# One PSUM bank for two heads' scores, and the FFN weights' residuals moved from GpSimd to VectorE

## The chip, the cores and the metric

The kernel runs on one core of a Trainium2 chip. A core has five engines that work beside each other, each through its own queue in order: TensorE (PE in the profile, with PEld for its weight loads), VectorE (DVE), ScalarE (ACT), GpSimd (POOL) and SyncE (SP), which here issues the DMAs. SBUF is the working memory; PSUM holds what PE writes, in banks of 512 fp32 columns on 128 partitions. The metric is the time of one execution in microseconds; the median of several executions is compared.

## What is computed

Three layers one after the other on 8 sequences of 576 tokens and 512 channels, all in fp32:

```python
# attention: 8 heads of 64, blocks of 64 positions, causal by block
scores = np.where(block_i >= block_j, q @ k.T / 8, -1e9)
x = softmax(scores) @ v                      # heads side by side: 576 x 512
# gated causal convolution of 5 taps
x = (sigmoid(conv5(x)) * (x @ w_val)) @ w_out
# Fourier mixing and a feed-forward layer
u = x + real(fft(fft(x, axis=1), axis=2))
un = (u - mean(u)) / sqrt(var(u) + 1e-6)
out = u + relu(un @ w_ch1) @ w_ch2           # 512 -> 2048 -> 512
```

## The kernel before

Products that must be exact to more than one rounded fp32 format are split: a value is rounded to a high part (`H`), the residual is its low part (`L`), and PE adds three matmuls, high x high, high x low and low x high.

`phase1` does attention, the gate and the Fourier stages. Its unit `n` is one of nine per head pair `p` (`p, i = divmod(n, NB)`): for `i` below 8 it is head `i % 2` and query tile `i // 2` of 128 queries; `i = 8` is the last 64 queries of both heads. A loop over `n` writes, in each round, the scores of unit `n` (`emit_qk`, two matmuls into a PSUM tile that `sc_tile` hands out), its masked maximum (`emit_max`), its exponents (`emit_exp`, on ACT, into `PB[i]`), six units later the transposes of the exponents (`emit_t`, line 487) and the product with `v` (`emit_av`, line 509). A score tile is one bank; three banks named `sc` go round (in the first 36 units two further ones help). Pieces of `dense`, the projections `psv` and `psx` and the Fourier matmuls of a batch of four head pairs, are strewn in between so that PE has work. Small stages that evacuate PSUM hang in chains that are run a step per round.

```python
t = sc_tile(n)
q = QQ[h][i // 4]
nc.tensor.matmul(t[:, 0:w], q[:, 0, m], KK[p][h][:, 0:w], start=True, stop=False)
nc.tensor.matmul(t[:, 0:w], q[:, 1, m], KL[p][:, 0:w], start=False, stop=True)
```

With `w = max(256, L)` and `L` 128 or 256, the first four units of a pair use half of their bank.

`phase2` is the feed-forward layer, in nine groups of 512 tokens. It reads the two weight matrices as 64-bit numbers; `load_w(f)` brings one of 16 slices of each as a raw tile `rw` (three buffers) and decodes it: three integer steps on DVE (lines 72, 74, 76) build the fp32 bits in `st` (three buffers), ACT takes the absolute value `mg` (line 80), DVE clears what is too small (line 84). Then ACT rounds `st` to `W1H` or `W2H` (line 962) and GpSimd subtracts to get `W1L` or `W2L` (line 963). `norm(g)` sums the four channel tiles of `U`, subtracts the mean, splits `x` into `UTH` and `UTL` (line 1015) and adds the squares `q` (line 1019). For each hidden tile `f`, PE makes `psh` from `W1` (lines 1049 to 1051), ACT the rectified high part `hh` (line 1054), DVE the low part `hl` (line 1055), and PE adds `W2` times both into four banks `o` (lines 1067 to 1069), one tile behind `psh`. In group 0 the decode of tile `f + 2` is written ahead of hidden tile `f`; `norm(g + 1)` runs inside group `g`. At a group's end DVE scales `o` and GpSimd adds it to `U` (line 1078).

The order on each queue is not that of the source: the tile framework's scheduler arranges the instructions of the whole program by its own estimate of when each can run, and places the semaphores. A queue waits in order, so an instruction that waits holds all behind it.

Of the kernel before, what the change touches and what calls it, by code (L numbers as in the profile page):

```python
# [8 lines left out]
F32 = mybir.dt.float32  # L9
F32R = mybir.dt.float32r  # L10
AF = mybir.ActivationFunctionType
ALU = mybir.AluOpType
AX = mybir.AxisListType
# [4 lines left out]
def kernel(  # L18
# [13 lines left out]
    nc = tc.nc  # L32
    B, NP, P, S = q.shape
# [66 lines left out]
    def phase1():  # L100
        with ExitStack() as c1:
# [4 lines left out]
            px, pv, pg, pool = (c1.enter_context(tc.tile_pool(name=f"p{n}", bufs=1)) for n in "xvgz")  # L106
# [12 lines left out]
            QQ = [[pa.tile([P, 2, 256], F32R, name=f"QQ{h}{g}") for g in range(2)] for h in range(2)]  # L119
# [23 lines left out]
            o = [0]  # L143
# [166 lines left out]
            qraw, kraw, KK, KP, KL, VV = {}, {}, {}, {}, {}, {}  # L310
# [62 lines left out]
                                      in_=QHL[rs[h], 0:1, c].bitcast(F32).to_broadcast([64, 2, 256]))  # L373
                    nc.sync.dma_start(out=QQ[h][g][rs[1 - h], 0, :].bitcast(F32), in_=QHL[rs[h], 1, c].bitcast(F32))

            sums, scs, maxs = {}, {}, {}

            sc_at = [0]

# [6 lines left out]

            def emit_qk(n):
                p, i = divmod(n, NB)
                if i < 8:

                    h, L = i % 2, P * (i // 2 + 1)
                    w = max(256, L)
                    m = slice(P * (i // 2 % 2), P * (i // 2 % 2) + P)
                    t = sc_tile(n)
                    q = QQ[h][i // 4]
                    nc.tensor.matmul(t[:, 0:w], q[:, 0, m], KK[p][h][:, 0:w], start=True, stop=False)  # L396
                    nc.tensor.matmul(t[:, 0:w], q[:, 1, m], KL[p][:, 0:w], start=False, stop=True)  # L397
                    scs[n] = [(t[:, 0:L], 0, L)]
                    return

                sc = []
                for k0, w in ((0, 320), (320, 256)):
                    t = sc_tile(n)
                    mm3(t[:, 0:w], QD[p % 2][:, 0], QD[p % 2][:, 1], KP[p][:, k0:k0 + w], KL[p][:, k0:k0 + w], True, True)
                    sc.append((t[:, 0:w], k0, w))
                scs[n] = sc

            def emit_max(n):
                sc = scs[n]
                mx = sm.tile([P, 4], F32, tag="mx", name="mx")  # L410
                one = len(sc) == 1
                if one:

                    L = sc[0][2]
                    nc.vector.memset(sc[0][0][0:64, L - 64:L], -1e9)
                for j, (t, k0, w) in enumerate(sc):
                    nc.vector.reduce_max(out=mx[:, j:j + 1], in_=t, axis=AX.X, negate=one)  # L417
                if not one:
                    nc.vector.reduce_max(out=mx[:, 2:3], in_=mx[:, 0:2], axis=AX.X, negate=True)
                maxs[n] = mx[:, 0:1] if one else mx[:, 2:3]  # L420
# [488 lines left out]
    def phase2():  # L909
        with ExitStack() as c2:  # L910
# [39 lines left out]
            def load_w(f):  # L950
                for src, h, l in (
                    (w_ch1[:, f * P:(f + 1) * P].bitcast(I32).rearrange("(c p) f -> p c f", p=P), W1H[f], W1L[f]),
                    (w_ch2[f * P:(f + 1) * P, :].bitcast(I32), W2H[f], W2L[f]),
                ):
                    rw = rp.tile([P, 2 * D], I32, tag="r", name="rw")
                    nc.sync.dma_start(out=rw if h is W2H[f] else rw.rearrange("p (c f) -> p c f", c=4), in_=src)
                    if h is W1H[f]:
                        h, l = h.rearrange("p c f -> p (c f)"), l.rearrange("p c f -> p (c f)")
                    st = s3.tile([P, D], F32, tag="st", name="st")
                    for stage in decode(rw, st, s4.tile([P, D], F32, tag="mg", name="mg")):  # L960
                        stage()
                    nc.scalar.copy(out=h, in_=st)  # L962
                    nc.gpsimd.tensor_tensor(out=l, in0=st, in1=h.bitcast(F32), op=ALU.subtract)  # L963

            U, UTH, UTL, RS = {}, {}, {}, {}

# [28 lines left out]
            def norm(g):  # L995
# [3 lines left out]
                UTH[g] = UHS[g % 2]  # L999
                UTL[g] = ULS[g % 2]  # L1000
                u = U[g]
                s1 = s2.tile([P, T], F32, tag="x", name="s1")
                s = s2.tile([P, T], F32, tag="x", name="s")
                nc.vector.tensor_tensor(out=s1, in0=u[:, 2, :], in1=u[:, 3, :], op=ALU.add)
                nc.gpsimd.tensor_tensor(out=s, in0=u[:, 0, :], in1=u[:, 1, :], op=ALU.add)
                nc.vector.tensor_tensor(out=s, in0=s, in1=s1, op=ALU.add)
                yield
                pm = ps_t.tile([P, T], F32, tag="t", name="pm")
# [2 lines left out]
                for t in range(4):  # L1011
                    x = s2.tile([P, T], F32, tag="x", name="x")
                    nc.vector.tensor_tensor(out=x, in0=u[:, t, :], in1=pm, op=ALU.subtract)
                    nc.scalar.copy(out=UTH[g][:, t, :], in_=x)
                    (nc.gpsimd if g and t % 2 else nc.vector).tensor_tensor(
                        out=UTL[g][:, t, :], in0=x, in1=UTH[g][:, t, :].bitcast(F32), op=ALU.subtract)
                    nc.scalar.activation(out=x if t else q, in_=x, func=AF.Square)
                    if t:
                        nc.gpsimd.tensor_tensor(out=q, in0=q, in1=x, op=ALU.add)
                    yield  # L1020
                pv = ps_t.tile([P, T], F32, tag="t", name="pv")
                yield from average(g, pv, q)
# [154 lines left out]
```

## Time and profile before

| | |
|---|---|
| median of three executions | 1527.51 us (1521.43 to 1528.04) |
| the profiled execution | 1526.26 us, of which the span of the trace is 1524.5 |
| TensorE | 1449.9 us busy, 95% of the span |
| VectorE | 859.1 us, 56% |
| ScalarE | 666.4 us, 44% |
| GpSimd | 393.1 us, 26% |
| granted TensorE clock, mean | 0.986 of full speed |

A busy share over the whole span hides that the stretches differ, so the rows below are asked for stretch by stretch. A duration is that of one instruction; on an engine with full work the distance from one start to the next is a little shorter than the duration, and it is this distance (the pitch) that adds up.

### The profile page before, as it was taken

To read this page: it belongs to the slowest core of one execution; us is meant where nothing else is said; L and a number is where in the kernel's file an instruction comes from. 1 tells how busy PE (TensorE), PEld (TensorE's weight loads), DVE (VectorE), ACT (ScalarE), POOL (GpSimd) and SP (SyncE) were. 2 spreads that over 40 slices of the span, in tenths; PEclk is the share of its full clock that TensorE was granted. 3 is DMA by queue.
4 is the path that set the end of the run, shared out by engine and by line. 5 is a ranking of instruction groups with operands and counts; after the bars stand their busy time and mean duration, and the time that the engine had idled before them with its cause. 6 is when DMAs were issued, how large, how long until landed. Compare 5 with 4: busy or idle time off the path is not lost.

```text
span 1524.5 us, 22867 instructions
## 1 busy us (share of the span) xinstructions
PE 1449.9 (95%) x8300; PEld 1213.1 (80%) x8300; DVE 859.1 (56%) x1798; ACT 666.4 (44%) x1674; POOL 393.1 (26%) x350
## 2 busy tenths in 40 slices
PE   4799999999999999988889999999999999999998
PEld 3477888888888888886667888888888888888887
DVE  6878797969796969599994222223222321322212
ACT  5678777777777777724342212112121211212110
POOL 3423332324232323245443112011111101111100
PEclk9899999999999999999999999999999999999999
DMA  7566555555454545224441010010101001010000
GB/s 205 159 166 186 145 143 131 143 133 147 125 148 121 153 116 137 87 74 136 144 137 56 1 52 4 1 56 0 56 0 55 1 2 53 0 56 1 28 1 28
DMA packets 114272, 129.12 MB, mean 85 GB/s; under 512 B 20208, under 2 KB 87792, under 8 KB 114160
## 3 DMA queue, kind: packets, MB, share of 16 engines
q1 hardware_dynamic: 114160, 127.67, 29.6%
q8 instruction: 66, 1.08, 0.3%
q14 instruction: 46, 0.38, 0.1%
HBM read 62.61 MB, written 18.87 MB: 53 GB/s over the span
## 4 chain that ended last, share of the span: by engine, by line
PE 80%; DVE 10%; DMA 3%; issue 3%; ACT 3%; POOL 1%; SPq 1%; DVEq 0%; ACTq 0%; POOLq 0%
PE o L1069 8%; PE o L1067 8%; PE o L1068 8%; PE psh L1050 8%; PE psh L1051 8%; PE psh L1049 8%; PE av L509 6%; PE pt L487 5%; PE sc L396 3%; PE sc L397 2%; PE psx L160 2%; PE psx L162 2%; PE psx L161 2%; DVE st L76 2%; PE psv L160 2%
## 5 line engine op out<-in xcount | busy, mean ns | idle before, releaser
L1055 DVE SCALAR_TENSOR_TENSOR hl<-psh,hh 128x512 fp32r<-128x512 f32 x144 | 99.2, 689 | 398.9 <-ACT hh L1054 398.9
L1054 ACT ACTIVATE hh<-psh 128x512 fp32r<-128x512 f32 x144 | 85.7, 595 | 494.8 <-PE psh L1051 494.8
L1069 PE MATMUL o<-hl,W2H 128*128 128x512 f32 x576 | 226.9, 395 | 16.6 <-DVE hl L1055 16.6
L1051 PE MATMUL psh<-UTH,W1L 128*128 128x512 f32 x576 | 224.7, 390 | 2.0 <-POOL W1L L963 2.0
L1067 PE MATMUL o<-hh,W2H 128*128 128x512 f32 x576 | 226.0, 393 | 0.0
L1068 PE MATMUL o<-hh,W2L 128*128 128x512 f32 x576 | 225.7, 392 | 0.0
L1049 PE MATMUL psh<-UTH,W1H 128*128 128x512 f32 x576 | 224.4, 390 | 0.3 <-ACT W1H L962 0.3
L1050 PE MATMUL psh<-UTL,W1H 128*128 128x512 f32 x576 | 224.2, 389 | 0.0
L430 ACT ACTIVATE PB<-sc,mx 128x128 f32<-128x128 f32 (+4 forms) x320 | 167.0, 524 | 47.9 <-DVE mx L417 40.8
L487 PE MATMUL pt<-ident,PB 128*128 128x128 f32 x800 | 139.1, 279 | 11.3 <-ACT PTb L492 4.2
L417 DVE TENSOR_REDUCE mx<-sc 128x1 f32<-128x128 f32 (+4 forms) x320 | 148.0, 473 | 2.7
L1069 PEld LDWEIGHTS o<-hl,W2H 128*128 128x128 f32 x576 | 109.1, 190 | 43.5 <-DVE hl L1055 21.0
L540 DVE SCALAR_TENSOR_TENSOR gate<-XF,cw,gate 128x575 f32<-128x575 f32 (+3 forms) x128 | 135.0, 1055 | 1.4 <-ACT gate L63 0.5
L1051 PEld LDWEIGHTS psh<-UTH,W1L 128*128 128x128 f32 x576 | 108.1, 188 | 25.5 <-POOL W1L L963 2.9
L1068 PEld LDWEIGHTS o<-hh,W2L 128*128 128x128 f32 x576 | 109.3, 190 | 22.9
L1067 PEld LDWEIGHTS o<-hh,W2H 128*128 128x128 f32 x576 | 109.1, 189 | 23.0 <-ACT hh L1054 0.2
L1049 PEld LDWEIGHTS psh<-UTH,W1H 128*128 128x128 f32 x576 | 108.4, 188 | 23.4 <-ACT W1H L962 0.7
L1050 PEld LDWEIGHTS psh<-UTL,W1H 128*128 128x128 f32 x576 | 108.1, 188 | 22.5
L396 PE MATMUL sc<-K,QQ 128*128 128x256 f32 (+2 forms) x256 | 92.6, 363 | 26.1 <-DMA QQ<-QHL 13.0
L487 PEld LDWEIGHTS pt<-ident,PB 128*128 128x128 f32 x800 | 99.5, 142 | 21.0 <-ACT PTb L492 7.1
L1078 POOL TENSOR_TENSOR U<-o,U 128x512 f32<-128x512 f32 x32 | 40.3, 1292 | 273.9 <-DVE o L1076 273.9
L492 ACT COPY PTb<-pt 128x512 f32<-128x512 f32 (+1 forms) x192 | 92.8, 501 | 31.2 <-PE pt L487 29.9
(184 smaller groups left out, 2931.7 us busy)
## 6 DMA issues: line engine op xcount, KB each, us to landing
K<-KP SPq DMA_DIRECT2D x128, 144.0 KB, 2.5
QQ<-QHL SPq DMA_DIRECT2D x128, 128.0 KB, 2.4
rw<-in_w_ch SPq DMA_DIRECT2D x32, 512.0 KB, 3.9
VV<-in_v SPq DMA_DIRECT2D x32, 320.0 KB, 3.8
qraw<-in_q SPq DMA_DIRECT2D x32, 288.0 KB, 3.0
kraw<-in_k SPq DMA_DIRECT2D x32, 288.0 KB, 3.1
out<-U SPq DMA_DIRECT2D x36, 256.0 KB, 2.0
QQ<-QHL SPq DMA_DIRECT2D x128, 64.0 KB, 2.1
```

The source lines that it names most:

```text
L396: nc.tensor.matmul(t[:, 0:w], q[:, 0, m], KK[p][h][:, 0:w], start=True, stop=False)
L417: nc.vector.reduce_max(out=mx[:, j:j + 1], in_=t, axis=AX.X, negate=one)
L430: nc.scalar.activation(out=PB[i][:, k0:k0 + w], in_=t, func=AF.Exp, bias=nm, accum_out=su[:, i + j:i + j + 1])
L487: nc.tensor.transpose(ps[:, j, :], PB[i][:, (j0 + j) * P:(j0 + j + 1) * P], ident)
L540: nc.vector.scalar_tensor_tensor(out=gate[c][:, s:S], in0=XF[:, 0:S - s], scalar=cw[:, c, 4 - s:5 - s], in1=gate[c][:, s:S], op0=ALU.mult, ...
L1049: nc.tensor.matmul(ps, W1H[f][:, c, :], UTH[g][:, c, :], start=(c == 0), stop=False)
L1050: nc.tensor.matmul(ps, W1H[f][:, c, :], UTL[g][:, c, :], start=False, stop=False)
L1051: nc.tensor.matmul(ps, W1L[f][:, c, :], UTH[g][:, c, :], start=False, stop=(c == 3))
L1055: nc.vector.scalar_tensor_tensor(out=l, in0=ps, scalar=0.0, in1=h.bitcast(F32), op0=ALU.max, op1=ALU.subtract)
L1067: nc.tensor.matmul(po[t], W2H[e][:, c], h, start=(e == 0), stop=False)
L1068: nc.tensor.matmul(po[t], W2L[e][:, c], h, start=False, stop=False)
L1069: nc.tensor.matmul(po[t], W2H[e][:, c], l, start=False, stop=(e == NF - 1))
```

## The change

Two things are changed. In `phase1`, the unit of head 0 (`i` 0 and 2) also does the scores of head 1, in the second half of the same bank; `emit_qk` of `i` 1 and 3 does nothing; one memset and one maximum with two results serve both heads, and `emit_max` of the second returns at once. The exponents stay one per head. In `phase2`, the residuals `W1L` and `W2L` are subtracted on DVE, and in `norm` of groups 0 and 1 the sum, the residuals `UTL` and the sum of squares are on DVE too; from group 2 on they stand where they stood.

```diff
             def emit_qk(n):
                 p, i = divmod(n, NB)
+                if i in (1, 3):
+
+                    return
                 if i < 8:
...
-                    q = QQ[h][i // 4]
-                    nc.tensor.matmul(t[:, 0:w], q[:, 0, m], KK[p][h][:, 0:w], start=True, stop=False)
-                    nc.tensor.matmul(t[:, 0:w], q[:, 1, m], KL[p][:, 0:w], start=False, stop=True)
-                    scs[n] = [(t[:, 0:L], 0, L)]
+                    for u in range(2 if i < 4 else 1):
+                        h, o = (u, w * u) if i < 4 else (i % 2, 0)
+                        q = QQ[h][i // 4]
+                        nc.tensor.matmul(t[:, o:o + w], q[:, 0, m], KK[p][h][:, 0:w], start=True, stop=False)
+                        nc.tensor.matmul(t[:, o:o + w], q[:, 1, m], KL[p][:, 0:w], start=False, stop=True)
+                        scs[n + u] = [(t[:, o:o + L], 0, L)]
+                    if i < 4:
+                        twos[n] = t.rearrange("p (h w) -> p h w", h=2)[:, :, 0:L]
...
             def emit_max(n):
+                if n in maxs:
+                    return
...
+                if n in twos:
+                    t = twos.pop(n)
+                    L = sc[0][2]
+                    nc.vector.memset(t[0:64, :, L - 64:L], -1e9)
+                    nc.vector.reduce_max(out=mx[:, 0:2], in_=t, axis=AX.X, negate=True)
+                    maxs[n], maxs[n + 1] = mx[:, 0:1], mx[:, 1:2]
+                    return
...
                     nc.scalar.copy(out=h, in_=st)
-                    nc.gpsimd.tensor_tensor(out=l, in0=st, in1=h.bitcast(F32), op=ALU.subtract)
+                    nc.vector.tensor_tensor(out=l, in0=st, in1=h.bitcast(F32), op=ALU.subtract)
...
+                pool = nc.gpsimd if g > 1 else nc.vector
...
-                nc.gpsimd.tensor_tensor(out=s, in0=u[:, 0, :], in1=u[:, 1, :], op=ALU.add)
+                pool.tensor_tensor(out=s, in0=u[:, 0, :], in1=u[:, 1, :], op=ALU.add)
...
-                    (nc.gpsimd if g and t % 2 else nc.vector).tensor_tensor(
+                    (pool if t % 2 else nc.vector).tensor_tensor(
...
-                        nc.gpsimd.tensor_tensor(out=q, in0=q, in1=x, op=ALU.add)
+                        pool.tensor_tensor(out=q, in0=q, in1=x, op=ALU.add)
```

On PE's queue, at the start of a head pair in the third batch, the scores of the two heads' first query tiles (`sc`, 128x256) stood eight rows apart before (`K_3395` is head 0, `K_3396` head 1; `PB` 119 and 120 are exponents of the pair ahead):

```order
L396 MATMUL sc<-K_3395,QQ_112 128x256
L397 MATMUL sc<-KL,QQ_112 128x256
L487 MATMUL pt<-ident,PB_119 128x128 x2
L160 MATMUL psv<-XH_132,wv_h 128x288
L161 MATMUL psv<-XL_137,wv_h 128x288
L162 MATMUL psv<-XH_132,wv_l 128x288
L160 MATMUL psv<-XH_133,wv_h 128x288
L161 MATMUL psv<-XL_138,wv_h 128x288
L162 MATMUL psv<-XH_133,wv_l 128x288
L396 MATMUL sc<-K_3396,QQ_114 128x256
L397 MATMUL sc<-KL,QQ_114 128x256
L487 MATMUL pt<-ident,PB_120 128x128 x3
```

and now (line numbers are those of the changed source):

```order
L401 MATMUL sc<-K_3291,QQ_112 128x256
L402 MATMUL sc<-KL,QQ_112 128x256
L401 MATMUL sc<-K_3292,QQ_114 128x256
L402 MATMUL sc<-KL,QQ_114 128x256
L503 MATMUL pt<-ident,PB_119 128x128 x2
L160 MATMUL psv<-XH_132,wv_h 128x288
L161 MATMUL psv<-XL_137,wv_h 128x288
L162 MATMUL psv<-XH_132,wv_l 128x288
L160 MATMUL psv<-XH_133,wv_h 128x288
L161 MATMUL psv<-XL_138,wv_h 128x288
L162 MATMUL psv<-XH_133,wv_l 128x288
L503 MATMUL pt<-ident,PB_120 128x128 x3
```

The second head's two matmuls moved up behind the first head's; the rows around them kept their order, and the next score tile is taken ten rows after the last one shown.

On DVE's queue, in the decode of two weight slices of group 0, before:

```order
L76 SCALAR_TENSOR_TENSOR st<-rw,st 128x512 x2
L84 SCALAR_TENSOR_TENSOR st<-mg,st 128x512 x2
L1055 SCALAR_TENSOR_TENSOR hl_9419<-psh,hh_9417 128x512
L72 TENSOR_SCALAR st<-rw 128x512
L1013 TENSOR_TENSOR x<-U_9485,pm 128x512
```

and now:

```order
L72 TENSOR_SCALAR st<-rw 128x512 x2
L74 SCALAR_TENSOR_TENSOR st<-rw,st 128x512 x2
L76 SCALAR_TENSOR_TENSOR st<-rw,st 128x512 x2
L84 SCALAR_TENSOR_TENSOR st<-mg,st 128x512 x2
L1073 SCALAR_TENSOR_TENSOR hl_9164<-psh,hh_9162 128x512
L979 TENSOR_TENSOR W1L_9202<-st,W1H_9201 128x512
L979 TENSOR_TENSOR W2L_9204<-st,W2H_9203 128x512
```

The two residuals moved into DVE's queue, behind the `hl` of an earlier hidden tile and ahead of the next slice's first step.

On ACT's queue in the same place, before:

```order
L962 CAST W1H_9457<-st 128x512
L80 ACTIVATE mg<-rw 128x512
L1054 ACTIVATE hh_9417<-psh 128x512
L962 CAST W2H_9459<-st 128x512
L80 ACTIVATE mg<-rw 128x512
```

and now:

```order
L1072 ACTIVATE hh_9161<-psh 128x512
L978 CAST W1H_9193<-st 128x512
L80 ACTIVATE mg<-rw 128x512
L978 CAST W2H_9195<-st 128x512
L80 ACTIVATE mg<-rw 128x512
L1072 ACTIVATE hh_9162<-psh 128x512
L978 CAST W1H_9197<-st 128x512
```

`hh`, which reads what PE made, moved ahead of the first of the two roundings.

## Rows read from the trace of the kernel before

**Rows 1.** Stretches, core 0: length, busy PE, PEld, DVE, ACT, POOL (count), PEclk, DMA, GB/s

```profile
100.00:657.00 557.00, 543.96 (x4187) 474.70 (x4182) 447.56 (x1164) 415.26 (x1168) 181.29 (x173) 1.00 0.51 136
657.00:717.00 60.00, 50.13 (x292) 43.52 (x291) 57.93 (x89) 24.39 (x47) 30.84 (x21) 0.94 0.28 96
717.00:804.00 87.00, 71.04 (x287) 54.90 (x286) 87.00 (x117) 36.88 (x64) 37.90 (x27) 0.96 0.45 149
804.00:1524.00 720.00, 715.71 (x3148) 591.60 (x3148) 194.28 (x252) 125.27 (x213) 106.66 (x79) 1.00 0.07 24
```

**Rows 2.** PE's waits, 100 to 650 us: total us, times, longest

```profile
PE sc L396 <- ACT PB L430: 11.8, 12, 2.4
```

**Rows 3.** Timeline 280 to 284 us, ACT and PE: start, length, [idle before <-releaser]

```profile
280.06 0.68 ACT L340 ACTIVATE QHL<-qraw 128x576 fp32r<-128x576 f32 x1 [1.67 <-DMA K<-KP]
...
281.30 0.39 PE L396 MATMUL sc<-K,QQ 128*128 128x256 f32 x1 [1.34 <-ACT PB L430]
...
281.64 0.49 PE L487 MATMUL pt<-ident,PB 128*128 128x128 f32 x3
...
283.89 0.30 PE L161 MATMUL psv<-XL,wv_h 128*128 128x288 f32 x1
```

**Rows 4.** DVE's groups by shape, 100 to 650 us: busy us, mean ns | idle before

```profile
L417 DVE TENSOR_REDUCE mx<-sc 128x1 f32<-128x512 f32 x54 | 37.1, 688 | 1.1
L417 DVE TENSOR_REDUCE mx<-sc 128x1 f32<-128x256 f32 x81 | 33.3, 411 | 0.2
...
L415 DVE MEMSET sc<- 64x64 f32 x215 | 24.0, 112 | 35.7 <-PE sc L397 28.3 <-PE pt L487 2.2 <-ACT KP L57 1.7
L417 DVE TENSOR_REDUCE mx<-sc 128x1 f32<-128x128 f32 x54 | 14.8, 274 | 0.0
```

**Rows 5.** PE's waits, 657 to 804 us

```profile
PE o L1069 <- DVE hl L1055: 16.6, 9, 3.2
```

**Rows 6.** DVE's groups by shape, 657 to 804 us

```profile
L76 DVE SCALAR_TENSOR_TENSOR st<-rw,st 128x512 int32<-128x512 int32 x32 | 32.6, 1027 | 0.0
L84 DVE SCALAR_TENSOR_TENSOR st<-mg,st 128x512 f32<-128x512 f32 x32 | 29.4, 926 | 0.0
L74 DVE SCALAR_TENSOR_TENSOR st<-rw,st 128x512 int32<-128x512 int32 x32 | 28.7, 903 | 0.0
L72 DVE TENSOR_SCALAR st<-rw 128x512 int32<-128x512 int32 x32 | 19.0, 602 | 0.0
```

**Rows 7.** Timeline of DVE, 718 to 722 us

```profile
718.48 0.41 DVE L72 TENSOR_SCALAR st<-rw 128x512 int32<-128x512 int32 x1
718.81 1.79 DVE L76 SCALAR_TENSOR_TENSOR st<-rw,st 128x512 int32<-128x512 int32 x1
720.52 0.68 DVE L74 SCALAR_TENSOR_TENSOR st<-rw,st 128x512 int32<-128x512 int32 x1
721.12 0.68 DVE L84 SCALAR_TENSOR_TENSOR st<-mg,st 128x512 f32<-128x512 f32 x1
```

**Rows 8.** Timeline of POOL, 718 to 722 us

```profile
718.68 1.37 POOL L963 TENSOR_TENSOR W2L<-st,W2H 128x512 fp32r<-128x512 f32 x1 [2.22 <-ACT W2H L962]
```

**Rows 9.** POOL's groups by shape, 657 to 804 us

```profile
L746 POOL TENSOR_TENSOR XA<-XA 128x580 f32<-128x580 f32 x6 | 9.7, 1616 | 5.9 <-DVE XA L746 5.9
```

**Rows 10.** ACT's groups by shape, 717 to 804 us

```profile
L80 ACT ACTIVATE mg<-rw 128x512 f32<-128x512 f32 x23 | 15.4, 669 | 1.5 <-DMA rw<-in_w_ch 1.5
...
L962 ACT CAST W1H<-st 128x512 fp32r<-128x512 f32 x12 | 7.4, 620 | 28.9 <-DVE st L84 28.9
L1054 ACT ACTIVATE hh<-psh 128x512 fp32r<-128x512 f32 x11 | 6.4, 579 | 0.0
```

**Rows 11.** Timeline of PE, 797 to 804 us

```profile
797.30 0.39 PE L1049 MATMUL psh<-UTH,W1H 128*128 128x512 f32 x1
797.53 0.39 PE L1050 MATMUL psh<-UTL,W1H 128*128 128x512 f32 x1
...
803.84 0.75 PE L1069 MATMUL o<-hl,W2H 128*128 128x512 f32 x1 [3.20 <-DVE hl L1055]
```

More of the change, by code (lines that the diff above doesn't have):

```diff
@@ L374, in spread @@
                     nc.sync.dma_start(out=QQ[h][g][rs[1 - h], 0, :].bitcast(F32), in_=QHL[rs[h], 1, c].bitcast(F32))
-            sums, scs, maxs = {}, {}, {}
+            sums, scs, maxs, twos = {}, {}, {}, {}
             sc_at = [0]
@@ L388, in emit_qk @@
                 p, i = divmod(n, NB)
+                if i in (1, 3):
+                    return
                 if i < 8:
-                    h, L = i % 2, P * (i // 2 + 1)
+                    L = P * (i // 2 + 1)
                     w = max(256, L)
```

## The prediction, made before the changed kernel was run

> **What bounds the kernel now.** I read the busy times by stretch first [rows 1]. The program has three parts. Until 657 us attention and the DFT stages of eight batches run, and TensorE (PE) is busy 544.0 of the 557 us after the start-up. From 657 to 804 the last batch drains and the first group of the feed-forward part decodes its weights; here VectorE (DVE) is busy 57.9 of 60 and then 87.0 of 87 us, while PE falls to 50.1 and 71.0. From 804 on PE is busy 715.7 of 720 us. So a time can be gained in two places only: where PE still waits in the first part, and in the 147 us in which DVE sets the pace.
>
> The view of PE's waits names both. Between 100 and 650 us almost all that PE waits for is a score tile that a softmax exponent has not yet left: 11.8 us in 12 waits [rows 2]. Between 657 and 804 it waits 16.6 us for `hl`, the residual that DVE makes after each hidden tile [rows 5]. From 804 on PE's 4.3 us of idle time are too little to matter, and GpSimd keeps its work there from group two on, so I change nothing after 804.
>
> **The scores.** For the first 256 queries the change replaces four memsets and four maxima per head pair by two and two. By the shapes [rows 4] the 128-wide pair costs 2 x 0.274 now and one 256-wide 0.411, which saves 0.137 us; the 256-wide pair 2 x 0.411 against one of 512 at 0.688 saves 0.134; two memsets save 0.224. That is 0.5 us per pair and 16 us over 32 pairs, all on DVE, which is busy 447.6 of 557 us there and does not set the end. I cost it at nothing.
>
> What counts is the tile. The trace shows the typical wait [rows 3]: at 281.30 PE issues the scores of the second head of a new pair after 1.34 us of waiting for an exponent. ACT could not run that exponent because its queue stood 1.67 us at `QHL`, behind a K copy by DMA. Before, the second head takes a buffer of its own, the one that the last 64 queries of the previous pair still hold. Now it goes into the half-empty bank of the first head, two rows after it in PE's order, and the next new tile is needed two transposes, one `av` and twelve projection matmuls later. That stretch was about 2.3 us long on PE, more than the 1.34 of the wait. Most of the 12 waits go, then: bounds 0 (PE meets the next late thing) and 11.8. The nearest row is the one at 281.30, which the new order outlasts, so I take 7. Costs on the other side: the first head's exponent now waits for the second head's scores, about 0.24 us of matmul, and the wider maximum, up to 0.28 us. PE needs the result six units later, so this is hidden in the steady part; in the first 100 us it could show: five pairs, two joint tiles each, 0.5 us, so at most 5 us lost, against shorter DVE work there. I take 0 and keep -3 to +5.
>
> **The decoding, what leaves GpSimd.** Every decode instruction of 128x512 on DVE is slowed when a GpSimd instruction runs beside it. At 720.52 and 721.12 they take 0.68 us and follow each other by 0.60; at 718.48 the first one, a shift, takes 0.41 and gives way after 0.33 [rows 7]. At 718.81 the same kind of instruction takes 1.79, under a GpSimd subtraction that ran from 718.68 for 1.37 [rows 7, 8]. The group means [rows 6] give the total: 32 x (1.027 + 0.926 + 0.903 - 3 x 0.68) + 32 x (0.602 - 0.41) = 26.1 + 6.1 = 32.2 us. In 717 to 804 DVE's 87.0 us hold 117 instructions [rows 1], which at the undisturbed pitches are 64 us (23 x 0.33 and 94 x 0.60), so 23 us of stretch stand against 27 GpSimd instructions, 0.85 each. Of the 48 GpSimd instructions between 657 and 804 about ten stay, the last batch's butterflies [rows 9] and four residuals; 38 go. They give back 38 x 0.85 = 32 us; with the mean over all 48 (32.2 / 48 = 0.67) it is 25. I take 30.
>
> The Trainium skill has a rule for this (SBUF — State Buffer, "Who interferes with whom"): where a DVE instruction has two inputs in SBUF and GpSimd reads SBUF, whichever issues second is held until the other is through. The rows at 718 agree with it in kind. By the rule's full hold, 38 x 1.37 = 52 us would go, where the measured stretch is 32.
>
> **What DVE gets instead.** Up to the `hl` of hidden tile 13, the last one that PE waited for (PE resumes at 803.84 after 3.20 us [rows 11]), DVE's new order holds 30 residuals of weights, two sums and four additions of squares more than before, 36 x 0.60 = 21.6. Of the rest one instruction fewer stands ahead of this `hl`, -0.6. Added: 21 us.
>
> **The wait that it adds.** Before, GpSimd waited for ACT's rounding of each weight; now DVE does, in its own queue, with the whole next tile's decode behind it. In ACT's new order from the seventh tile on, `hh` of the previous hidden tile stands just ahead of that rounding, so DVE waits for ACT, ACT for PE, and PE for an earlier `hl`. The loop, over two tiles: from the end of an `hl`, PE finishes ten matmuls of `o` and twelve of `psh`, 22 x 0.23 = 5.0 [rows 11], plus 0.2 for the last one to land; ACT does `hh` 0.58, the rounding 0.62, the next absolute value 0.67 and the second rounding 0.62 [rows 10]; then DVE 0.60 for the residual, 0.67 and seven times 0.60 until the `hl` two tiles on. Together 13.2, or 6.6 per tile. DVE alone needs 2 x 0.33 + 9 x 0.60 = 6.1. So each of nine tiles waits about 0.5: 4 us. Where the last batch drains, two of these residuals stand behind copies of DFT results and one behind the square root: an estimate of 3 us from the same ACT rows. Bounds for all such waits: 1 and 12 (if the nine tiles ran at 7.4).
>
> Sum for this part: -30 + 21 + 7 = -2, and -4 with 32 given back; I take -3. With the bounds of the terms it runs from -10 to +8. DVE is busy throughout, so what it gains or loses PE gains or loses, as long as PE's own 24 matmuls per tile (24 x 0.23 = 5.5) stay under DVE's 6.1, which they do.
>
> **Rivals.** *The loop eats the gain.* The nine tiles run at 7 us and not 6.6, and the decode is worth nothing: 1527.5 - 7 = 1520.5. For it: ACT is in order and the absolute value stands between the two roundings. Against: DVE has the other slice's clearing step and an `hl` to do, 1.2 us, before it needs the first rounding.
> *The score waits only move.* PE arrives earlier and waits for transposes or for a scale: 1527.5 - 3 = 1524.5. For it: ACT's stall on the K copy stays where it is. Against: ACT and DVE are each busy under 81% there [rows 1]. Both together give 1527.5.
> *A full hold.* If each of the 38 gives back 1.11 us, the largest stretch (1.79 - 0.68), 42 us go, and the part gains 42 - 21 - 7 = 14, most of what PE waits for `hl`: 1527.5 - 7 - 14 = 1506.5. The group means speak against it. This is what the skill's rule of the full hold points to.
> *Slower: the loop at half clock.* PE's granted clock is 0.96 of full in 717 to 804 [rows 1], so for some of the time, while PE waited much, it stood at the lower of its two levels (1.2 and 2.4 GHz). If it stays there inside the loop, the 22 matmuls take 5 us more and a tile, half a loop, costs 9.1 and not 6.6. Nine such tiles lose 22 us: 1517.5 + 22 = 1539.5. It comes out over 0.5% slower from about seven of the nine tiles on.
>
> **How the numbers follow.** The profiled execution took 1526.3 us (span 1524.5 and 1.8 around it), 1.2 under the median of 1527.5. The forecast is 1526.3 - 7 - 3 = 1516.3 in its terms, 1517.5 in the median's. Chances: forecast 0.43 (own range 1511 to 1523), loop eats the gain 0.20, waits only move 0.17, both 0.08, full hold 0.05, slower 0.07. To leave out no more than two in ten, the range runs from 1509 to 1528. About 0.5%, 7.6 us, is what a measurement of this kernel can tell from no change. Below 1519.9 lie the full hold, about 0.35 of the forecast's 0.43, half of the loop's rival, which stands at that bound, and a little of the other: 0.52. Slower is 0.07, and the rest 0.41.
>
> **What would show it.** Right: between 100 and 650 us PE waits for score tiles 2 to 5 us, not 11.8; in the decode no DVE instruction of 128x512 but those beside the last batch's butterflies takes over 0.7 us; `hl` of the hidden tiles comes every 6.1 to 6.8 us; DVE now shows idle time ended by ACT's rounding, some 4 to 7 us; the last `hl` that PE waits for comes near 794 us, 10 earlier, of which 7 are the first part's. Wrong: PE's waits in the first part are as long as before under another name; the tiles come every 7 us or more; or the first 100 us are longer by several us.

## The result, and the profile after

The changed kernel takes 1508.84 us (median of 4 runs, 1506.37 to 1511.09) against 1527.78 (1521.43 to 1529.35) for the kernel before in the runs beside it: ratio 0.9883, 95% interval 0.985 to 0.9917. That is 18.9 us less; the prediction was 10. Its range, 1509 to 1528 against a kernel before of 1527.5, is 0.988 to 1.000 as a ratio, and 0.9883 lies just inside; the time itself is 0.2 us under 1509.

Where the 15.9 us between the two profiled spans come from is read best from a few moments of each trace (us from the start of the span; a pair's values begin with the first matmul `av<-PTb`, and `hl` is taken at its end on DVE):

| moment | before | after | gained so far |
|---|---|---|---|
| values of the 1st head pair | 30.7 | 28.3 | 2.4 |
| of the 10th | 213.2 | 211.0 | 2.2 |
| of the 30th | 608.5 | 600.1 | 8.4 |
| of the 32nd | 643.8 | 636.1 | 7.7 |
| first shift of the decoding (DVE, line 72) | 657.7 | 650.0 | 7.7 |
| `hl` of hidden tile 13 | 803.8 | 788.9 | 14.9 |
| `hl` of hidden tile 15 | 812.1 | 795.9 | 16.2 |
| end | 1524.5 | 1508.6 | 15.9 |

So about half comes from the attention part and half from the decoding, and nothing from the rest, as the prediction's shape had it: it put 7 on the attention part and 3 on the decoding. The busy times by stretch of the changed kernel (columns as in [rows 1]):

```profile
100.00:657.00 557.00, 544.57 (x4228) 480.58 (x4229) 451.45 (x1067) 412.09 (x1164) 183.95 (x175) 1.00 0.52 138
657.00:717.00 60.00, 49.46 (x265) 41.19 (x264) 58.31 (x98) 26.18 (x51) 10.85 (x8) 0.91 0.34 114
717.00:804.00 87.00, 78.51 (x325) 61.29 (x326) 83.67 (x145) 40.16 (x69) 2.54 (x2) 0.98 0.38 129
```

GpSimd went from 48 instructions in the last two stretches to 10. PE's waits between 100 and 650 us (total, times, longest) answer to [rows 2]:

```profile
PE rt L472 <- ACT PTa L508: 7.1, 6, 1.7
PE rt L472 <- POOL XF L460: 2.9, 2, 2.6
PE sc L401 <- ACT PB L446: 1.3, 4, 0.4
```

The 11.8 us of score waits are down to 1.3, but 10 us of waits for `rt`, the transposes of the reciprocal sums, stand in their place. By this view alone one would say that nothing was gained, and yet the pairs come faster: from the 10th to the 30th in 389.1 us, before in 395.3. The decode groups of DVE between 657 and 804 us answer to [rows 6] (1.027, 0.926, 0.903 and 0.602 us there):

```profile
L74 DVE SCALAR_TENSOR_TENSOR st<-rw,st 128x512 int32<-128x512 int32 x32 | 23.2, 742 | 0.0
L84 DVE SCALAR_TENSOR_TENSOR st<-mg,st 128x512 f32<-128x512 f32 x32 | 22.6, 724 | 0.0
L76 DVE SCALAR_TENSOR_TENSOR st<-rw,st 128x512 int32<-128x512 int32 x32 | 21.9, 703 | 0.0
L72 DVE TENSOR_SCALAR st<-rw 128x512 int32<-128x512 int32 x31 | 13.8, 460 | 0.1
L979 DVE TENSOR_TENSOR W2L<-st,W2H 128x512 fp32r<-128x512 f32 x16 | 10.9, 682 | 0.0
L979 DVE TENSOR_TENSOR W1L<-st,W1H 128x512 fp32r<-128x512 f32 x16 | 10.9, 682 | 0.0
L1073 DVE SCALAR_TENSOR_TENSOR hl<-psh,hh 128x512 fp32r<-128x512 f32 x16 | 10.9, 681 | 0.8 <-ACT hh L1072 0.8
```

The last two numbers of a row are the point: the residuals cost their 0.68 us, and neither they nor the rest show idle time ended by ACT's rounding. Every decode instruction that is still lengthened stands beside the last batch's butterflies and residuals on GpSimd, ahead of 703 us.

### The profile page after: what moved, and what is told of

The parts are those of the page before. It is cut to its first block, busy times and chain, and to the rows that moved or that the text cites. A ratio compares the mean times of both kernels' runs of the same rounds, so it can differ in the third digit from the quotient of the medians.

```text
span 1508.6 us, 22589 instructions
## 1 busy us (share of the span) xinstructions
PE 1442.5 (96%) x8300; PEld 1212.7 (80%) x8300; DVE 851.2 (56%) x1712; ACT 663.7 (44%) x1674; POOL 331.4 (22%) x308
## 4 chain that ended last, share of the span: by engine, by line
PE 82%; DVE 10%; ACT 2%; issue 2%; DMA 2%; POOL 1%; SPq 1%; ACTq 0%; DVEq 0%; POOLq 0%
PE psh L1068 8%; PE psh L1069 8%; PE psh L1067 8%; PE o L1087 8%; PE o L1085 8%; PE o L1086 8%; PE av L525 6%; PE pt L503 5%; PE sc L401 2%; PE psx L160 2%; PE sc L402 2%; PE psx L162 2%; PE psx L161 2%; PE psv L160 2%; PE psv L161 2%
## 5 line engine op out<-in xcount | busy, mean ns | idle before, releaser
L1073 DVE SCALAR_TENSOR_TENSOR hl<-psh,hh 128x512 fp32r<-128x512 f32 x144 | 99.3, 690 | 398.3 <-ACT hh L1072 398.3
L1087 PE MATMUL o<-hl,W2H 128*128 128x512 f32 x576 | 220.8, 394 | 15.5 <-DVE hl L1073 15.4
L556 DVE SCALAR_TENSOR_TENSOR gate<-XF,cw,gate 128x575 f32<-128x575 f32 (+3 forms) x128 | 127.2, 994 | 2.4 <-ACT gate L63 2.3
L433 DVE TENSOR_REDUCE mx<-sc 128x1 f32<-128x384 f32 (+2 forms) x192 | 104.4, 561 | 2.4 <-PE sc L162 0.2
L401 PE MATMUL sc<-K,QQ 128*128 128x256 f32 (+2 forms) x256 | 87.3, 351 | 13.8 <-DMA QQ<-QHL 12.5
```

The lines of the kernel that those rows point to most:

```text
L401: nc.tensor.matmul(t[:, o:o + w], q[:, 0, m], KK[p][h][:, 0:w], start=True, stop=False)
L556: nc.vector.scalar_tensor_tensor(out=gate[c][:, s:S], in0=XF[:, 0:S - s], scalar=cw[:, c, 4 - s:5 - s], in1=gate[c][:, s:S], op0=ALU.mult, ...
L1073: nc.vector.scalar_tensor_tensor(out=l, in0=ps, scalar=0.0, in1=h.bitcast(F32), op0=ALU.max, op1=ALU.subtract)
L1087: nc.tensor.matmul(po[t], W2H[e][:, c], l, start=False, stop=(e == NF - 1))
```

## Experiments

Every kernel ran beside the kernel before on its own chip; ratios are to that. A table first, since the text goes back to it. The last three columns, in us: the moment of the first pair's values, the time from the values of the 10th pair to those of the 30th, and that from the first shift of the decoding to the `hl` of tile 13.

| kernel | median us, ratio [95%] | 1st pair | 10th to 30th | decoding |
|---|---|---|---|---|
| before | 1526.3 to 1527.8 | 30.7 | 395.3 | 146.1 |
| after | 1508.8, 0.9883 [0.985, 0.9917] | 28.3 | 389.1 | 138.9 |
| scores_alone | 1517.2, 0.9928 [0.9911, 0.9945] | 28.9 | 389.1 | 145.7 |
| decode_alone | 1518.1, 0.993 [0.991, 0.995] | 32.6 | 396.4 | 137.6 |
| bank_shared_only | 1553.9, 1.0176 [1.0147, 1.0205] | 32.2 | 413.5 | 145.5 |
| moved_up_only | 1525.0, 0.9989 [0.9977, 1.0002] | 30.4 | 394.6 | 146.0 |
| joint_bank_two_maxima | 1532.2, 1.0037 [1.0019, 1.0056] | 38.5 | 394.9 | 145.8 |
| late_two_maxima | 1523.9, 0.999 [0.9977, 1.0004] | 28.1 | 395.5 | 145.7 |
| third_transpose_bank | 1527.3, 1.001 [0.9995, 1.0024] | 39.5 | 398.3 | 143.2 |
| q_on_gpsimd | 1511.7, 0.991 [0.9895, 0.9925] | 28.3 | 389.9 | 139.5 |
| ten_matmuls_after_hl | 1512.9, 0.9908 [0.9885, 0.9931] | 28.5 | 389.8 | 139.5 |
| late_hh | 1512.9, 0.9917 [0.9894, 0.9939] | 27.4 | 389.9 | 140.0 |
| idle_gpsimd_work | 1533.4, 1.0047 [1.0028, 1.0065] | 28.6 | 390.8 | 163.0 |
| residuals_alone | 1523.9, 0.9977 [0.9961, 0.9993] | 31.2 | 396.8 | 141.1 |

The time from the 10th to the 30th pair is the steadiest measure here: the three kernels with the scores as before show 395.3 to 396.8, the six with the change's scores and banks 389.1 to 390.8.

**The two halves apart.** `scores_alone` undoes lines 979 and 1019 to 1037 of the change, `decode_alone` undoes `emit_qk` and `emit_max`.

> Only the scores part of the change: joint tile, joint maximum; the feed-forward part as before. Theory (each edit acts in its own part and the two gains add): the 32nd pair's values are reached about 7.7 us earlier than before (636 instead of 643.8), as in the changed kernel, and the time is 1527.8 - 8 = 1520; PE's score waits are about 1 us and some 7 to 10 us of waits for rt stand in their place; the decoding still takes 146 us from its first shift to the hl of tile 13. Rival (the whole gain is the decoding's, the score waits only moved): 1525 to 1528, and the decoding alone near 1511.

> Only the decoding part of the change: weight residuals and the sums of groups 0 and 1 on VectorE; the scores as before. Theory: the stretch from the first shift to the hl of tile 13 takes 139 instead of 146 us, hl comes every 6.2 us, PE's order there has the four hl matmuls at the end of each tile as in the changed kernel, and the time is 1527.8 - 8 = 1520 (1517 to 1522). PE's 12 us of score waits stay. Rival (the gain is the scores'): 1526 to 1529. If the two parts did not add, the two runs' gains would sum to something far from 18 us.

Measured: 9.5 and 8.6 us by the medians, 18.1 together, and 18.9 for the whole change. The halves add. `decode_alone` keeps the waits for score tiles of the kernel before, `scores_alone` has those of the changed kernel and the decoding of the one before (145.7). PE's waits, 100 to 650 us, first of `decode_alone`, then of `scores_alone`:

```profile
PE sc L396 <- ACT PB L430: 12.5, 13, 1.9
...
PE rt L472 <- ACT PTa L508: 6.8, 9, 1.5
...
PE sc L401 <- ACT PB L446: 1.4, 4, 0.5
```

**What in the scores gains.** The prediction said the bank, and that DVE's shorter work is worth nothing.

```diff
 # bank_shared_only: the second head at its old place, in the same tile, own memset and maximum
+t = twos[n] if n in twos else sc_tile(n)
+if i in (0, 2): twos[n + 1] = t
 # moved_up_only: both heads issued together, each in a tile of its own
+for u in range(2 if i < 4 else 1):
+    t = sc_tile(n + u)
 # joint_bank_two_maxima: the change's tile, but
-nc.vector.memset(t[0:64, :, L - 64:L], -1e9)
-nc.vector.reduce_max(out=mx[:, 0:2], in_=t, axis=AX.X, negate=True)
+for u in range(2):
+    nc.vector.memset(t[0:64, u, L - 64:L], -1e9)
+    nc.vector.reduce_max(out=mx[:, u:u + 1], in_=t[:, u], axis=AX.X, negate=True)
 # late_two_maxima: this last edit only from the seventh head pair on
```

> Both heads' scores of the first 256 queries share a bank, but the second head's matmuls stay at their old place and each head keeps its own memset and maximum; the feed-forward part as before. Theory (what counts is the score bank saved): the gain of the scores alone within 2 us, 1520, PE's score waits under 4 us. Rival (the gain comes from the matmuls moved up or from DVE's shorter maxima): 1526 to 1528 with the 12 us of waits still there.

> The second head's scores are issued right behind the first head's, but in a bank of their own and with maxima of their own; the feed-forward part as before. Theory (bank): two banks are wanted at once, so PE's score waits stay at 12 us or grow; 1527 to 1535. Rival (moving the matmuls up is what helps): 1520 to 1522.

> The run with the bank shared but the second head left at its old place came out 27 us slower, since its scores waited for the first head's maximum of the same bank. Here both heads' scores are issued together into the joint bank, but each head keeps its own memset and maximum (the DVE work of before); the feed-forward part as before. Theory (the bank saved is the gain, the merged maximum is only DVE work that nobody waits for): as the scores alone, 1517 (1515 to 1520), PE's score waits under 4 us. Rival (the shorter work on DVE is part of the gain): 1521 to 1526, with score waits of 6 us or more.

> As the joint bank with two maxima, but the first six head pairs keep the one maximum of the change, so that the start-up stays as in the scores alone. Theory (the bank is the gain; the two maxima cost only through the order of work in the first 40 us): the first pair's values at 28 to 30 us, the 32nd at about 637, time as the scores alone, 1517 (1515 to 1519). Rival (the merged maximum is worth something in the steady part): 1521 or more, with the 32nd pair later than 640.

`moved_up_only` came out as the theory had it: moving the matmuls up is worth nothing. `bank_shared_only` decides nothing: it is 27 us slower, and new waits came with it. PE's waits, 100 to 650 us:

```profile
PE rt L462 <- POOL XF L450: 12.2, 7, 1.9
PE sc L400 <- DVE mx L423: 9.6, 14, 2.2
PE sc L400 <- ACT PB L436: 7.0, 9, 2.5
```

In the second row the second head's scores are held until DVE has read the first head's from the same tile. The first row, the largest, is a wait for GpSimd's copy of the reciprocals (0.8 us in `decode_alone`); what brought it stays open. So this run is no case for sharing a bank when one head is read before the other is written.

The two runs with both heads written first and two maxima then contradict the theory. `late_two_maxima` starts like the changed kernel (28.1), shows only 3.6 us of score waits, and still needs 395.5 us for the twenty pairs, what the kernel before needs. One maximum instead of two, with the order that the planner makes of it, is worth 6 of them. What the waits view hides shows when I add up, over those twenty pairs, by how much each start-to-start time of PE's matmuls exceeds the usual one of its kind and width with the same kind behind it (the 20th percentile over nine of the runs), by what PE turns to next:

| PE turns to | before | late_two_maxima | scores_alone |
|---|---|---|---|
| scores, from projections | 8.9 | 2.5 | 0.1 |
| `rt`, from transposes | 1.7 | 6.1 | 7.3 |
| anything else, with a score, transpose or projection on either side | 5.2 | 6.7 | 2.0 |
| together | 15.8 | 15.3 | 9.4 |

(Products with `av`, projections and `rt` among themselves are left out; they differ by under 1.5 us.) With the shared bank alone 6.4 us go from the waits for scores, and 5.9 come back behind them. With the joint maximum the first and third rows shrink by 7 us more. DVE's timeline shows what the second maximum costs, first in `late_two_maxima`, then in `scores_alone`:

```profile
297.17 0.11 DVE L425 MEMSET sc<- 64x64 f32 x1
297.20 1.41 DVE L656 CAST XOOH<-XA 128x290 fp32r<-128x290 f32 x1
298.53 0.28 DVE L426 TENSOR_REDUCE mx<-sc 128x1 f32<-128x128 f32 x1
298.73 1.37 DVE L557 SCALAR_TENSOR_TENSOR gate<-XF,cw,gate 128x573 f32<-128x573 f32 x1
300.11 0.11 DVE L425 MEMSET sc<- 64x64 f32 x1
300.14 0.81 DVE L557 SCALAR_TENSOR_TENSOR gate<-XF,cw,gate 128x572 f32<-128x572 f32 x1
300.87 0.28 DVE L426 TENSOR_REDUCE mx<-sc 128x1 f32<-128x128 f32 x1
...
296.46 0.17 DVE L424 MEMSET sc<- 64x128 f32 x1
296.54 1.33 DVE L655 CAST XOOH<-XA 128x290 fp32r<-128x290 f32 x1
297.79 0.41 DVE L425 TENSOR_REDUCE mx<-sc 128x2 f32<-128x256 f32 x1
```

In DVE's order other work of 0.8 to 1.4 us stands between the steps of one tile, the taps of the gate above all. Two memsets and two maxima give it three such places, one of each gives it one: here 4.0 us from the first memset to the last maximum's end against 1.7, over the twenty pairs 3.1 against 1.7 in the mean. The exponents of the first joint tile start 4.4 and 4.6 us after their scores with two maxima and 2.9 and 3.4 with one.

DVE alone does not explain that. With two maxima the first head's own is through 2.4 us after its scores, with the joint one 2.8, and yet its exponents then start 2.0 us later against 0.1. The planner had moved them in ACT's order too. ACT, first in `late_two_maxima`, where the first head's maximum had ended at 298.81, then in `scores_alone`:

```profile
297.93 0.71 ACT L340 ACTIVATE QHL<-qraw 128x576 fp32r<-128x576 f32 x1
...
301.05 0.69 ACT L581 ACTIVATE gate<-gate 128x576 f32<-128x576 f32 x1 [0.17 <-DVE gate L557]
301.64 0.35 ACT L447 ACTIVATE PB<-sc,mx 128x128 f32<-128x128 f32 x1
...
298.30 0.37 ACT L446 ACTIVATE PB<-sc,mx 128x128 f32<-128x128 f32 x1 [0.96 <-DVE mx L425]
298.65 0.68 ACT L340 ACTIVATE QHL<-qraw 128x576 fp32r<-128x576 f32 x1
```

In this place the exponents stand ahead of `QHL` with one maximum, and wait for DVE; with two they stand behind it and four more instructions. DVE's queue delays the second head's maximum, from 2.6 to 3.9 us after its scores, and ACT's order delays the first head's exponents. What I priced at 0.5 us of busy DVE per pair was 1.2 to 1.5 us of delay in the exponents, but how the 6 us divide between the two queues, and which of PE's later waits they end, no run shows: none has two maxima with ACT's order of the joint one.

`joint_bank_two_maxima` came out another 8 us slower by the medians. The queues of PE, ACT and GpSimd between the 10th and the 30th pair have the order of `late_two_maxima`; what differs lies at the start, where its first pair's values come at 38.5 us, 10.4 later, of which 3.7 are left at the 32nd pair and 6.6 at the end of the profiled executions. There the planner put two steps of the value weights' decoding ahead of the first reciprocals on GpSimd, whose copy starts at 29.6 us and not at 20.6, and PE waits for it:

```profile
30.03 0.48 PE L473 MATMUL rt<-ident,XF 128*128 128x128 f32 x1 [3.43 <-POOL XF L461]
```

**Is a bank to spare now?** PE's new waits are for `rt`, which shares two banks with the other transposes.

```diff
 # third_transpose_bank: ps_sc bufs 3 -> 2, ps_pt bufs 2 -> 3
 # q_on_gpsimd, in q_hi:
-nc.scalar.activation(out=QHL[:, 0, :], in_=qraw[p], func=AF.Copy, scale=0.125)
+if p < 6:
+    nc.scalar.activation(out=QHL[:, 0, :], in_=qraw[p], func=AF.Copy, scale=0.125)
+else:
+    nc.gpsimd.tensor_scalar_mul(out=QHL[:, 0, :], in0=qraw[p], scalar1=0.125)
```

> The changed kernel with the bank that the joint tile frees given away: two banks of their own for scores instead of three, three for transposes instead of two. Theory (the waits for rt are the old waits at the next scarce bank, behind ACT's stall at QHL): the 7 us of rt <- PTa go, score waits stay under 4 us, time 1502 to 1506. Rival (the scores still need three): score waits of 6 us or more come back, 1509 to 1518.

> The changed kernel with the scaled and rounded queries (QHL) made by GpSimd instead of ACT from the seventh head pair on, so that a late copy out of QHL no longer holds ACT's queue. Theory (TensorE's remaining waits for rt are ACT's stall at QHL, the one that made it wait for score tiles before): rt <- PTa falls from 7.1 us to under 3, time 1502 to 1506. Rival (the stall moves on to GpSimd, whose copy of the reciprocals stands behind it): rt <- XF grows from 2.9 to 8 us or more, 1509 to 1516.

The rival holds for the bank: `rt <- PTa` is gone, and 12.2 us of waits for tiles of whole heads (7.2 for the first joint tile of a pair, 5.2 for the third query tile) and 5.6 for the last queries' stand there. With two banks of their own the joint tiles are slower (398.3) than the separate ones with three:

```profile
PE sc L401 <- ACT PB L446: 12.2, 12, 3.7
PE sc L160 <- ACT PB L446: 5.6, 7, 0.9
```

So the spared bank is needed by the change, as far as this one plan tells, though by itself it gained nothing. The first pair of this run also came late, at 39.5, by the same other order on GpSimd at the start (first copy at 29.8). For the queries neither side is right: `rt <- PTa` falls to 4.8 us (7 times) and `rt <- XF` stays at 2.9, and the time is no better than the changed kernel's. The stall at `QHL` is at most a part of what the transposes wait for. No version tried was faster than the change.

**The contention by itself.**

```diff
 # idle_gpsimd_work, behind each residual
+nc.gpsimd.tensor_tensor(out=idle, in0=h.bitcast(F32)[:, 0:448], in1=h.bitcast(F32)[:, 64:512], op=ALU.subtract)
```

> The changed kernel with work that nobody needs: after each of the 32 rounded weight tiles GpSimd subtracts 128x448 of it from itself into a tile that nobody reads. Nothing waits for GpSimd there, so only what it does to a DVE instruction beside it can show. Theory (the give-back is contention, 0.85 us for each 128x512 operation): 0.74 us for each, two per tile, hl every 7.6 us and not 6.15, 30 x 0.74 = 22 more: 1531 (1526 to 1536). Rival (full hold, each stops DVE for its own 1.2 us): 30 x 1.2 = 36, 1545. Rival (the gain came from waits between engines that the change removed): at most 3 us more, 1512.

Measured: 24.6 us more, and `hl` of the steady tiles every 7.73 us instead of 6.15, so 0.79 us for each operation that nobody waits for. The give-back is contention. The rows tell more than the mean; GpSimd first, then DVE:

```profile
738.87 1.15 POOL L981 TENSOR_TENSOR idle<-W1H 128x448 f32<-128x448 f32 x1 [5.03 <-ACT W1H L979]
740.10 1.49 POOL L981 TENSOR_TENSOR idle<-W2H 128x448 f32<-128x448 f32 x1
...
738.60 0.68 DVE L1075 SCALAR_TENSOR_TENSOR hl<-psh,hh 128x512 fp32r<-128x512 f32 x1
739.20 1.37 DVE L980 TENSOR_TENSOR W1L<-st,W1H 128x512 fp32r<-128x512 f32 x1
740.49 1.64 DVE L980 TENSOR_TENSOR W2L<-st,W2H 128x512 fp32r<-128x512 f32 x1
```

GpSimd's first operation ends at 740.02 and `W1L` at 740.57; the second at 741.59 and `W2L` at 742.13. Each DVE residual ends 0.55 us after the GpSimd operation beside it, whatever its own start, and so did the row at 718.81 of the kernel before, which ends at 720.60, 0.55 after GpSimd's 720.05 [rows 7, 8]. `hl`, which reads one of its inputs from PSUM, runs its 0.68 us with GpSimd beside it. So the hold is a full one, but its price is only what is left of the GpSimd operation when DVE comes to its next instruction of that kind: at the most 1.11 before, about 0.8 in the mean. And it falls on DVE only where GpSimd was first. Of the 57 decode instructions that overlap one of GpSimd between 657 and 804 us of the kernel before, GpSimd had begun first beside 41, and 36 of these are lengthened, by 0.89 us in the mean; beside the other 16 DVE had begun first, and none is. So "every decode instruction is slowed" in the prediction says too much.

The Trainium skill states the halves (SBUF — State Buffer, "Who interferes with whom": two SBUF inputs contend with GpSimd's reads; at most one, outside DVE's two-port modes, doesn't; the first to issue keeps the shared ports for its whole instruction, and the other is blocked). The rows of the residuals and of `hl` agree. The shift of line 72 has one input and is held as well (0.602 us in the mean against 0.41 [rows 6, 7]); whether it ran in a two-port mode no run here shows. What I made of the rule in the prediction, a loss of the whole 1.37 per operation, was not what it says.

**The wait that did not come.**

```diff
 # ten_matmuls_after_hl: in group 0, but for the last hidden tile, for t = 1, 2, 3 the product with hl stands first
-order of a tile's products: (W2H, hh), (W2L, hh), (W2H, hl)
+order of a tile's products: (W2H, hl), (W2L, hh), (W2H, hh)
 # late_hh: in group 0
+for _ in range(5):
     nc.scalar.activation(out=h, in_=ps, func=AF.Relu)
```

> The changed kernel with one thing moved: in the first feed-forward group TensorE multiplies by hl first for the last three of the four output tiles, so that ten matmuls of o stand between an hl and the next psh, as I had assumed, and not four. Theory (the loop of the forecast is real and only TensorE's order hid it): hl of tiles 2 to 8 comes every 6.6 us and not 6.2, DVE shows idle time ended by ACT's rounding, and the time is 1508.8 + 4 = 1513. Rival (DVE's 6.15 us per tile set the pace in either order): spacing 6.15 to 6.3, time 1507 to 1510.

> The changed kernel with hh of the first feed-forward group computed five times over by ACT, so that it comes about 2 us later; TensorE's order keeps its four hl matmuls at the end of a tile, and the five stand partly ahead of either rounding. Theory (the loop through hl, psh, hh, the second rounding and DVE's residual exists, and the change runs just under it): from the end of an hl 16 matmuls 3.7, landing 0.2, five hh 2.55, two roundings and an absolute value 1.7, then DVE 5.5 to the end of the hl two tiles on: 13.7 or 6.85 per tile instead of 6.15, and the time 5 to 8 us more, 1514 to 1517. Rival (DVE's own work sets the pace with room to spare): hl stays at 6.15 to 6.3, 1509 to 1511.

Neither brought the loop. With ten matmuls `hl` of tiles 2 to 8 comes every 6.14 to 6.56 us, 6.2 in the mean; with five `hh` every 6.08 to 6.27. In both the planner answered the edit with another order elsewhere. ACT in `ten_matmuls_after_hl`:

```profile
737.81 0.62 ACT L978 CAST W1H<-st 128x512 fp32r<-128x512 f32 x1 [2.81 <-DVE st L84]
738.33 0.66 ACT L80 ACTIVATE mg<-rw 128x512 f32<-128x512 f32 x1
738.90 0.61 ACT L978 CAST W2H<-st 128x512 fp32r<-128x512 f32 x1
739.41 0.59 ACT L1072 ACTIVATE hh<-psh 128x512 fp32r<-128x512 f32 x1
```

`hh` moved behind both roundings, where it holds up nothing. In `late_hh` it stands partly ahead of either, but four decode steps now stand ahead of DVE's residual of W2, and four, not eight, between it and the next `hl`. Medians of 1512.9 for both are 4 us over the changed kernel's, and the intervals of the ratios overlap with its; by the traces 0.6 and 1.1 of them lie in the decoding.

**Which of the moved operations.**

> Only the residuals of the decoded weights go to VectorE; the sums of groups 0 and 1 stay on GpSimd, the scores as before. Theory (each operation moved gives back about 0.80 to 0.85 us of stretched DVE time and costs 0.60): about 30 of them ahead of the hl of tile 13, 30 x -0.22 = -6.6, so 1526.8 - 6.6 = 1520; the other eight operations are worth the remaining 2 us of the decoding's 8.6. Rival (the sums of the norm, which stand in the way of the square root and the first tiles, carry the gain): 1524 to 1527.

Only line 979 of the change is kept here. Inconclusive: by the trace the decoding takes 5.0 us less than before, of 7.2 to 8.5 with the sums of groups 0 and 1 moved as well; by the medians only 2.4 of 8.6. In its profiled run the stretch from the 1st pair to the 32nd, whose instructions and their order on each queue are those of before, took 617.3 us against 613.1. So much two runs of the same code differ there, and a gain of 5 us in one place is told by the moments of a trace rather than by three medians.

## Why the prediction was right in its sign and short in its size

**The scores: the size holds, the reason fell.** Forecast -7; by the trace -7.7 at the 32nd pair, by the medians of `scores_alone` -9.5. One pair of traces is a rough measure: with the scores of before the 32nd pair comes at 643.8, 647.8 and 648.5 us, with the change's in five traces at 636.1 to 638.9, the means 9.7 apart. The first 100 us, forecast at 0, moved by 0.4 at the fifth pair. But the step "all on DVE, which does not set the end: I cost it at nothing" was wrong, and with it "what counts is the tile". The spared bank alone gains nothing (`late_two_maxima`); the rival that the waits only move describes it well. Merging the two maxima makes the difference of 6 us, by the exponents' earlier start and not by DVE's busy time as such; whether DVE's queue or ACT's order, which changed with it, carries it stays open. So the 7 came out near the measured size by luck: it was worked out from a stretch on PE that, by itself, gave nothing. Of the signs named, PE's waits for score tiles fell further than the 2 to 5 us, to 1.3; the sign of being wrong, as much wait under another name, came true with 10.0 for 11.8, and the pairs were faster all the same.

**The decoding: the size failed, and it is the mis-sized term.** Forecast -3; measured -7.2 in the traces and -8.6 in the medians of `decode_alone`. The give-back of 30 is borne out (0.79 per operation against 0.85, and DVE's instructions beside a GpSimd one exceed their undisturbed lengths by 36.8 us between 657 and 804 us before and by 7.4 between 649 and 797 now, 29 less), and so is the added 21 (32 residuals at 0.68 of length, 0.60 of pitch). The term that failed is the wait, +7: it is 0 to 1. Between 709 and 789 us DVE is busy 79.9 of 80 us, and of the 4 to 7 us that it was to wait for ACT's rounding there is nothing. DVE's waits in the changed kernel, 649 to 797 us:

```profile
DVE XA L762 <- POOL XA L762: 1.7, 2, 1.0
DVE hl L1073 <- ACT hh L1072: 0.8, 1, 0.8
DVE XOOH L655 <- ACT XA L649: 0.6, 1, 0.6
```

The loop was put together from ACT's order of after and PE's order of before. PE's order changed in the same plan. Before, ten matmuls of `o` stand from the first with `hl`, at 803.84 [rows 11], to the next `psh`:

```profile
807.60 0.39 PE L1069 MATMUL o<-hl,W2H 128*128 128x512 f32 x1
807.83 0.40 PE L1049 MATMUL psh<-UTH,W1H 128*128 128x512 f32 x1
```

Now the four products with `hl` stand together at the end of a tile (PE, then ACT, then DVE):

```profile
742.02 1.19 PE L1087 MATMUL o<-hl,W2H 128*128 128x512 f32 x4 [0.56 <-DVE hl L1073]
743.05 0.40 PE L1067 MATMUL psh<-UTH,W1H 128*128 128x512 f32 x1
...
745.98 0.60 ACT L1072 ACTIVATE hh<-psh 128x512 fp32r<-128x512 f32 x1 [2.19 <-PE psh L1069]
746.93 0.62 ACT L978 CAST W1H<-st 128x512 fp32r<-128x512 f32 x1 [0.36 <-DVE st L84]
...
746.22 1.29 DVE L84 SCALAR_TENSOR_TENSOR st<-mg,st 128x512 f32<-128x512 f32 x2
747.42 0.68 DVE L1073 SCALAR_TENSOR_TENSOR hl<-psh,hh 128x512 fp32r<-128x512 f32 x1
```

So four and not ten matmuls of `o` stand ahead of the next `psh`, six times 0.23 less, and my loop comes to 13.2 - 1.4 = 11.8 or 5.9 per tile, under the 6.15 at which DVE delivers. `hh` is through 0.36 us before the rounding can start, which waits for DVE and not the other way. `hl` comes every 6.1 to 6.3 us from tile 2 to 8, as DVE alone would have it, and then at 7.3, 6.7, 6.1, 6.7 and 7.9 up to tile 13, with DVE busy all the time; the last `hl` that PE waits for comes at 788.9, where 794 was named. Whether the loop can pace this kernel at all stays open: in none of the runs it did, since an edit that should bring it made the planner sort the other engines anew.

**The rivals.** Loop eats the gain: no. Waits only move: true of the bank alone, not of the change. Full hold: its 1506.5 lies closest to the result of all, but by chance; each operation gave back about 0.8 and not 1.11, and the rest came from the wait that is not there. Loop at half clock: no; the granted clock of 717 to 804 is 0.98, before 0.96.

**The sum mended.** 1526.3 - 7.7 (scores) - 7.2 (decoding to tile 13) - 1.3 (on to tile 15) + 0.3 (the rest) = 1510.4 in the terms of the profiled execution.

## What to carry to other kernels

A small step on an engine that is 80% busy need not be free when it stands in a chain between two others: look at its place in that engine's queue, and at where the planner then puts the step that waits for it, and not at its busy time alone. Where a planner orders all engines at once, a loop through several of them has to be read from all their orders in the same plan, and an edit made to test one link may dissolve it. When waits move from one name to another, measure the pace between two repeated events, and not the sum of the waits.

## What was not expected of the hardware

A DVE instruction with two inputs in SBUF ended 0.55 us after the GpSimd operation beside it in all three places shown (720.60, 740.57 and 742.13), though the operations lasted 1.37, 1.15 and 1.49 us and DVE had issued 0.13, 0.33 and 0.39 us behind their start; so did all 29 two-input decode instructions that are lengthened between 657 and 804 us of the kernel before. The one-input shift beside them ended 0.28 us after. And the first 40 us are fragile: two kernels whose edits lie in the scores began about 10 us later (38.5 and 39.5 us against 27.4 to 32.6 in all others), and in both GpSimd's queue has two steps of the weights' decoding ahead of the first copy of the reciprocals (29.6 and 29.8 us against 20.6 in `scores_alone` and `late_two_maxima`).
